# Three value blocks of one head group per layer, stored on forty partitions and loaded by eight five-row transfers

## The chip, the cores and the metric

The kernel runs on one core of one Trainium2 chip. The metric is the device time of one execution in microseconds, as the median of several runs; the kernel before takes 2583.27 us. A profile of one execution, with a record of every instruction and every DMA packet, is the source of all other numbers.

## What is computed

One decode step (one new token, batch of two) goes through two layers. Each layer is an attention block over a long key and value cache followed by a gated feed-forward block, and both layers use the same caches and weights:

```
x = x + attention(layernorm(x), k_cache, v_cache, wq, wo)   # 32 query heads, 8 key heads, 32768 keys, 128 wide, float32
x = x + ((relu(h @ W_gate) * (h @ W_up)) @ W_down), h = layernorm(x)
(both lines once more)

q = (h @ wq) as [2, 32 heads, 1, 128];  scores = q . k / sqrt(128);  p = softmax(scores);  o = p . v;  o @ wo
```

The caches are 2 x 8 x 32768 x 128 floats each, 268 MB for the keys and 268 MB for the values. They do not fit on the chip's on-core memory, so each layer reads all of them.

## The kernel before

**Tiling.** There are 16 head groups (8 key heads times 2 batch rows). A group's keys are two tiles of 128 partitions x 16384 floats (8 MB each), its values as well. Such a tile is four pages of 128 x 4096 floats (2 MB), and a page is eight blocks of 128 x 512 floats, so a group has 8 pages and 64 value blocks. Layer 0 takes the groups in order 0 to 15, layer 1 from 15 to 0.

**Loop.** In a layer, step i multiplies the queries with the keys of group i (`keys(i)`, matmuls at line 219 into `sc`), then the probabilities of group i-1 with its values (`values(i-1)`, line 263 into `acc`). The softmax of group i is split: `soft_max` (line 227) after the first value page, `soft_tail` (line 242: transposes the probabilities to `pT`, sums them) after the second key page of the next step. `head_out` and `project` add a group's output through `wo` to `op`. After group 15 come the feed-forward block (`wgu`, `wd`) and, in layer 0, the queries of layer 1 (`wq`).

**Memory and loads.** All loaded data and most scratch live in one tile, `arena`, 220 units of 1 KB per partition. `take` picks the free units that have been free longest, `done` gives units back. A load (line 73) is one DMA that SyncE (SP) issues in program order; each waits until the work that used its units has ended. Besides, a load waits for the eighth load before it: there are eight completion semaphores (DMAHW0 to DMAHW7 in the order of the program), used in turn, and one is used again only when its last transfer has landed on all sixteen DMA engines. A load of 8 MB is usually issued two or three tiles ahead of its use. A tile with 128 rows is spread evenly over the 16 DMA engines, eight rows each.

**Ends of the layers.** Layer 0 keeps the keys of its last group, and some pages of its values, for layer 1, which starts with the same group; the arena has then less room, and the values of its last two groups are loaded in pages of 2 MB (or 16 KB per row), not tiles of 8 MB. In layer 1 only the very last group's values are loaded in pages. `selq` is a small constant (128 rows of 128 bytes), loaded near the end of layer 0 by six transfers of 2, 3, 5, 6, 7 and 105 rows (lines 409 to 411).

Of the kernel before, what the change touches and what calls it, by code (L numbers as in the profile page):

```python
# [7 lines left out]
F32 = mybir.dt.float32  # L8
# [4 lines left out]
P = 128  # L13
D = 512
HKV, REP, DH, SK = 8, 4, 128, 32768
NB = 2
F = 1792
NG = HKV * NB
NT = 8
# [5 lines left out]
NLAYER = 2  # L25
# [12 lines left out]
KEPT_PART, KEPT_FROM = 3, 6  # L38
DOWN = (4, 4, 2, 2, 1, 1)

C_SAME, C_MEAN, C_SELH, C_PAIR, C_COL, C_SELQ, C_END = 0, 128, 256, 272, 304, 306, 338

SELQ_ROWS = (0, 2, 5, 10, 16, 23, 128)


@with_exitstack
def attention_reglu_decode(ctx: ExitStack, tc: tile.TileContext, x, k, v, wq, wo, wgu, wd, consts, out):
# [53 lines left out]

    xq = sb.tile([P, P], F32, name="x")
    nc.scalar.dma_start(xq, x)
    cst = sb.tile([P, C_SELQ], F32, name="cst")
    nc.scalar.dma_start(cst, consts[:, :C_SELQ])
    selq = sb.tile([P, C_END - C_SELQ], F32, name="selq")
    same = cst[:, C_SAME : C_SAME + P]
    selh = cst[:, C_SELH : C_SELH + 16]
    pair = cst[:, C_PAIR : C_PAIR + 32]
    mean_rows = cst[:, C_MEAN : C_MEAN + P]  # L110
    col = cst[:, C_COL : C_COL + NB]

    mean_cols = sb.tile([P, 1], F32, name="ones")
# [7 lines left out]
    acc = ps.tile([P, D], F32, name="acc")  # L121
# [86 lines left out]
        nc.vector.tensor_copy(qz[:, i % 2, 28 : 28 + REP], qT[:, REP * hk : REP * hk + REP, b])  # L208


    sc_of, pT_of, linv_of, red_of = {}, {}, {}, {}

    def k_tile(L, i, n, j, kt):
        if j == 0:
# [24 lines left out]
        nc.scalar.activation(p[0], sc_of[n].rearrange("p a b -> p (a b)"), AF.Exp, bias=nm[:, 0:1], scale=1.0, accum_out=rs)  # L239
        red_of[n] = (p, rs)  # L240

    def soft_tail(L, n):
        p, rs = red_of.pop(n)
        pT = take(2 * D)
        for B in range(2):
            nc.vector.transpose(pT[0][:, B * D : (B + 1) * D], p[0][:, B * D : (B + 1) * D])  # L246
        done(p)
        sm = small(f"sm{L}_{n}")
        nc.tensor.matmul(sm[:, 0:1], same, rs, start=True, stop=True)  # L249
        linv = one()  # L250
        nc.vector.reciprocal(linv, sm[:, 0:1])  # L251
        pT_of[n], linv_of[n] = pT, linv

# [93 lines left out]
    for L in range(NLAYER):  # L347
        last = L == NLAYER - 1
        seq = list(range(NG)) if L % 2 == 0 else list(range(NG - 1, -1, -1))

        def keys(i):
            n = seq[i]
            if i < NG - 1:
                place_queries(i + 1, seq[i + 1])
            if last and i == 0:
                loads = list(kept_k)
                kept_k.clear()
            else:
                loads = pages(k, n, not (last and i == 1))
            for j, t in enumerate(loads):  # L360
                k_tile(L, i, n, j, t[0])
                if not last and i == NG - 1:
                    kept_k.append(t)
                else:
                    done(t)
                if last and i == 0:
                    yield
                if j == 1 and i >= 1:
                    soft_tail(L, seq[i - 1])
                if j == 2 and i >= 2:  # L370
                    head_out(L, seq[i - 2])
                    if i % 2 == 1:
                        project(load(wo[seq[i - 2] // NB], True), i == 3, False)


        def values(i, soft):
            n = seq[i]
            whole = (j for j in ())
            if i == NG - 1:
                pieces = [(j, 0, 8, None) for j in range(NT - 1)]  # L380
                pieces += [(NT - 1, h, h + 2, None) for h in range(0, 8, 2)]
                if not last and KEPT_FROM < 8:
                    pieces[KEPT_PART : KEPT_PART + 1] = [(KEPT_PART, 0, KEPT_FROM, None), (KEPT_PART, KEPT_FROM, 8, None)]
            elif last and i == 0:
                pieces = kept_v[1:] + kept_v[:1]
                pieces += [(j, 0, 8 if j != KEPT_PART else KEPT_FROM, None) for j in range(NT) if j not in KEPT_PAGES]
                kept_v.clear()
            else:
                pieces = [(j, 0, 8, None) for j in range(NT)]
                whole = pages(v, n, last or i < NG - 2)  # L390
            for at, (j, lo, hi, t) in enumerate(pieces):
                t = t or next(whole, None) or load(v[n, j // HALF, :, j % HALF * PAGE + lo * D : j % HALF * PAGE + hi * D])
                v_tile(n, j, t[0], at == 0, j == NT - 1, range(lo, hi))
                if not last and i == NG - 1 and (j in KEPT_PAGES or j == KEPT_PART and lo):
                    kept_v.append((j, lo, hi, t))
                else:
                    done(t)
                if soft is not None and at == 0:
                    soft_max(L, soft)
            evacuate(L, n, i == NG - 1)  # L400

        first_keys = keys(0)
        queries(L, total, seq[0], first_keys if last else iter(()))
        list(first_keys)
        soft_max(L, seq[0])
        for i in range(1, NG):
            list(keys(i))
            values(i - 1, seq[i])
            if i == NG - 2 and not last:
                for lo, hi in zip(SELQ_ROWS, SELQ_ROWS[1:]):  # L410
                    nc.sync.dma_start(selq[lo:hi], consts[lo:hi, C_SELQ:])
        soft_tail(L, seq[NG - 1])
        head_out(L, seq[NG - 2])
        values(NG - 1, None)
# [48 lines left out]
```

## Time and profile before

| | us |
|---|---|
| median of three runs (2582.8 to 2583.68) | 2583.27 |
| the profiled execution | 2581.4 |
| its span, first to last instruction | 2579.5 |
| TensorE busy (matmul) | 1299.9 |
| VectorE busy | 143.5 |
| time of DMA packets on the main queue, as a share of 16 engines over the span | 99.5% |

The span is what the trace shows; the profiled execution has 1.9 us around it, and it is 1.9 us under the median. The profile's views used here are the page, the chain of work that ended last, tables of stretches (busy time, DMA share), the timeline, what SP's queue waited for, and DMA packets by queue in a stretch. The DMA share of a stretch is the mean busy share of the 16 DMA engines; packets are counted in the stretch in which they start, so a share can stand a little over 1.

### The profile page before, as it was taken

How to read it: one execution, taken by the hardware profiler on the slowest of the kernel's cores; microseconds unless marked ns; L12 is line 12 of the kernel's file. 1: busy time of each engine (PE TensorE's matmuls, PEld its weight loads, DVE VectorE, ACT ScalarE, POOL GpSimd, SP SyncE). 2: the span in 40 equal slices, each digit the busy share in tenths (PEclk: the TensorE clock that was granted, in tenths of full speed). 3: DMA queues.
4: the chain of work that ended last, by engine and by line, in shares of the span. 5: the costliest groups of instructions: out<-in, count | busy, mean ns of one | idle time of the engine just before them, and what ended most of it. 6: DMA issues, size and time to landing. Idle time of an engine off the chain costs nothing.

```text
span 2579.5 us, 20070 instructions
## 1 busy us (share of the span) xinstructions
PE 1299.9 (50%) x9544; PEld 343.3 (13%) x9544; DVE 143.5 (6%) x341; ACT 42.0 (2%) x69; POOL 3.0 (0%) x11
## 2 busy tenths in 40 slices
PE   2554554455445444545575554445445544554456
PEld 0111111111111111111111111111111101111111
DVE  0000000000000000000010000000000000000000
ACT  0000000000000000000000000000000000000000
POOL 0000000000000000000000000000000000000000
PEclk9777777777777777777878677777777776777778
DMA  9999999999999999999999999999999999999998
GB/s 425 428 434 434 432 429 435 431 435 431 428 438 434 425 437 434 430 431 427 407 409 436 432 433 431 433 435 427 434 436 428 432 436 430 432 432 432 435 424 371
DMA packets 30776, 1107.33 MB, mean 429 GB/s; under 512 B 3558, under 2 KB 3942, under 8 KB 7142
## 3 DMA queue, kind: packets, MB, share of 16 engines
q1 hardware_dynamic: 30406, 1105.82, 99.5%
q8 instruction: 75, 1.23, 0.2%
q10 hardware_dynamic: 288, 0.22, 0.0%
q14 instruction: 7, 0.06, 0.0%
HBM read 1105.96 MB, written 0.07 MB: 429 GB/s over the span
## 4 chain that ended last, share of the span: by engine, by line
DMA 67%; PE 23%; another core or an unknown queue 10%; issue 0%; DVE 0%; ACTq 0%; SPq 0%; DVEq 0%
DMA arena<-k 54%; PE sc L219 16%; DMA arena<-v 7%; PE acc L263 5%; DMA cst<-consts 2%; DMA arena<-wgu 1%; DMA arena<-wd 1%; PE po L287 1%; DMA arena<-wq 1%; PE op L169 1%; PE qp L189 1%; PE mp L233 0%; PE sm L249 0%; PE gu L306 0%
## 5 line engine op out<-in xcount | busy, mean ns | idle before, releaser
L263 PE MATMUL acc<-arena 128*16 128x512 f32 x4136 | 587.7, 720 | 606.4 <-DMA arena<-v 606.3
L219 PE MATMUL sc<-arena,qz 128*32 128x512 f32 x4096 | 590.2, 728 | 592.9 <-DMA arena<-k 592.9
L219 PEld LDWEIGHTS sc<-arena,qz 128*32 128x32 f32 x4096 | 144.0, 130 | 986.0 <-issue 668.4
L263 PEld LDWEIGHTS acc<-arena 128*16 128x16 f32 x4136 | 119.2, 109 | 1025.7 <-DMA arena<-v 513.5
L229 DVE TENSOR_REDUCE stat<-sc 128x1 f32<-128x1024 f32 x32 | 39.2, 1225 | 656.9 <-PE sc L219 656.9
L239 ACT ACTIVATE arena<-sc,stat 128x1024 f32<-128x1024 f32 x32 | 35.6, 1113 | 2374.0 <-DVE stat L236 2322.1
L281 DVE TENSOR_SCALAR arena<-acc,stat 128x512 f32<-128x512 f32 x30 | 22.5, 751 | 732.9 <-PE acc L263 732.9
L246 DVE STREAM_TRANSPOSE arena<-arena 128x512 f32<-128x512 f32 x64 | 41.5, 687 | 2.5 <-ACT arena L239 2.5
L287 PE MATMUL po<-cst,arena 128*128 128x4 f32 x256 | 33.9, 255 | 2.4 <-DVE arena L278 1.2
L287 PEld LDWEIGHTS po<-cst,arena 128*128 128x128 f32 x256 | 31.1, 191 | 27.0 <-issue 23.5
L251 DVE RECIPROCAL stat<-sm 128x1 f32<-128x1 f32 x32 | 5.3, 166 | 422.6 <-PE sm L249 422.6
L306 PE MATMUL gu<-arena 128*32 128x448 f32 x128 | 23.3, 840 | 10.7 <-DMA arena<-wgu 9.9
L236 DVE TENSOR_REDUCE stat<-mp 128x1 f32<-128x32 f32 x32 | 6.1, 192 | 358.0 <-PE mp L233 358.0
L189 PE MATMUL qp<-arena 128*32 128x512 f32 x128 | 20.1, 735 | 8.3 <-DMA arena<-wq 6.7
L142 PE MATMUL meana<-stat,cst 128*128 128x1 f32 x4 | 0.9, 304 | 43.4 <-DMA cst<-consts 42.9
L233 PEld LDWEIGHTS mp<-arena,cst 128*128 128x128 f32 x64 | 13.0, 253 | 52.1 <-issue 45.3
L169 PE MATMUL op<-arena,oT 128*2 128x128 f32 x512 | 17.7, 281 | 4.1 <-DVE oT L290 4.1
L233 PE MATMUL mp<-arena,cst 128*128 128x32 f32 x64 | 16.9, 352 | 3.2 <-DVE arena L232 3.2
L249 PEld LDWEIGHTS sm<-stat,cst 128*128 128x128 f32 x64 | 9.5, 188 | 27.6 <-issue 27.6
L169 PEld LDWEIGHTS op<-arena,oT 128*2 128x2 f32 x512 | 12.1, 86 | 6.0 <-DVE oT L290 5.5
L249 PE MATMUL sm<-stat,cst 128*128 128x1 f32 x64 | 12.2, 260 | 0.0
L290 DVE COPY oT<-po 128x4 f32<-128x4 f32 x32 | 5.2, 161 | 77.2 <-PE po L287 77.2
(51 smaller groups left out, 71.2 us busy)
## 6 DMA issues: line engine op xcount, KB each, us to landing
arena<-v SPq DMA_DIRECT2D x25, 2048.0 KB, 34.3
arena<-wo SPq DMA_DIRECT2D x16, 1024.0 KB, 50.5
arena<-k SPq DMA_DIRECT2D x8, 2048.0 KB, 14.2
arena<-wq SPq DMA_DIRECT2D x8, 1024.0 KB, 7.1
arena<-wgu SPq DMA_DIRECT2D x8, 896.0 KB, 8.5
arena<-wgu SPq DMA_DIRECT2D x4, 1792.0 KB, 21.0
arena<-v SPq DMA_DIRECT2D x9, 512.0 KB, 28.0
arena<-wd SPq DMA_DIRECT2D x4, 1024.0 KB, 7.8
```

The source lines that it names most:

```text
L169: nc.tensor.matmul(tot[32 * c : 32 * c + rows.shape[-1], :P], rows, w[:, c * P : (c + 1) * P], start=start, stop=stop)
L189: nc.tensor.matmul(qp[32 * c : 32 * c + 32, B, :], xT[:, kt, :], t[0][:, c * D : (c + 1) * D], start=kt == 0, stop=kt == KT - 1)
L219: nc.tensor.matmul(sc_of[n][32 * c : 32 * c + 32, B, :], qz[:, i % 2, 28 - 4 * j : 60 - 4 * j], kt[:, ch * D : (ch + 1) * D], start=j == 0 ...
L229: nc.vector.tensor_reduce(m1, sc_of[n], AX.XY, ALU.max)
L233: nc.tensor.matmul(mp[:, :32], same, mt[0], start=True, stop=True)
L239: nc.scalar.activation(p[0], sc_of[n].rearrange("p a b -> p (a b)"), AF.Exp, bias=nm[:, 0:1], scale=1.0, accum_out=rs)
L246: nc.vector.transpose(pT[0][:, B * D : (B + 1) * D], p[0][:, B * D : (B + 1) * D])
L249: nc.tensor.matmul(sm[:, 0:1], same, rs, start=True, stop=True)
L263: nc.tensor.matmul(acc[32 * c : 32 * c + 16, e * w : (e + 1) * w], pT[:, B, m, 16 * J : 16 * J + 16], vt[:, at * D + e * w : at * D + (e + ...
L281: nc.vector.tensor_scalar_mul(acs, acc, linv[:, 0:1])
L287: nc.tensor.matmul(po[:, :REP], acs[0][:, t * P : (t + 1) * P], selh[:, 4 * t : 4 * t + 4], start=t == 0, stop=t == 3)
L306: nc.tensor.matmul(gu[32 * j : 32 * j + 32, s, :FS], xT[:, kt, :], t[0][:, j * FS : (j + 1) * FS], start=kt == 0, stop=kt == KT - 1)
```

## The change

In each layer one group (the one at step 14 of 16, `i == NG - 2`) has three of its 64 value blocks taken out of the ordinary layout: blocks 4, 5 and 6 of page 3. Their 384 keys, padded to 400, are stored a second time in a new input, `side`, as 40 rows of 20,480 bytes: ten chunks of 40 keys. They stand on partitions 0 to 19 and 32 to 51 of the arena, and eight transfers of five rows (every fourth partition) load them, between the first and the second page of that group. Page 3 is then loaded in two parts, blocks 0 to 3 and block 7. The group's other pages are loaded one by one in both layers (in layer 1 they were two tiles of 8 MB).

The probabilities of these keys need another layout as well: `side_keys` makes it in `soft_tail` of that group with three transposes and one multiplication on VectorE and one memset on GpSimd, and `v_side` adds ten matmuls into `acc` after the first value page. `selq` becomes a part of `cst`, and its six transfers go.

```diff
-SELQ_ROWS = (0, 2, 5, 10, 16, 23, 128)
+SIDE_PAGE, SIDE_AT, SIDE = 3, 4, 3
+SIDE_ROWS, SIDE_CHUNKS = 20, 5
...
-    cst = sb.tile([P, C_SELQ], F32, name="cst")
-    nc.scalar.dma_start(cst, consts[:, :C_SELQ])
-    selq = sb.tile([P, C_END - C_SELQ], F32, name="selq")
+    cst = sb.tile([P, C_END], F32, name="cst")
+    nc.scalar.dma_start(cst, consts)
...
-    def soft_tail(L, n):
+    def soft_tail(L, n, aside=False):
...
+        if aside:
+            side_of[n] = side_keys(p[0])
...
+    def side_keys(p):
+        W = SIDE_CHUNKS * 32
+        t = take(2 * W)
...
+        nc.gpsimd.memset(t[0][64:, W:], 0.0)
+        nc.vector.transpose(chunks(t[0][:, :W]), windows(p))
+        for c in (0, 32):
+            nc.vector.transpose(chunks(t[0][c : c + 32, W:]), windows(p[64 + c : 96 + c]))
+        nc.vector.tensor_scalar_mul(t[0], t[0], side_rows[:, 0:1])
+        return t
+
+    def v_side(n, vt):
+        t = side_of.pop(n)
+        J = SIDE_PAGE // 4
+        for k in range(2 * SIDE_CHUNKS):
+            nc.tensor.matmul(
+                acc[32 * (k % 4) : 32 * (k % 4) + 16, :],
+                t[0][:, 32 * k + 16 * J : 32 * k + 16 * J + 16],
+                vt[:, k * D : (k + 1) * D],
+                start=False, stop=False,
+            )
+        done(t)
+
+    def load_side(n):
+        t = take(2 * SIDE_CHUNKS * D, False, False)
+        for c in (0, 32):
+            for r in range(4):
+                nc.sync.dma_start(t[0][c + r : c + SIDE_ROWS : 4], side[n, c // 32, r])
+        return t
...
+            elif i == NG - 2:
+                pieces = [(0, 0, 8, None)]
+                for j in range(1, NT):
+                    if j == SIDE_PAGE:
+                        pieces += [(j, 0, SIDE_AT, None), (j, SIDE_AT + SIDE, 8, None)]
+                    else:
+                        pieces.append((j, 0, 8, None))
...
+                if i == NG - 2 and at == 1:
+                    t_side = load_side(L)
+                    v_side(n, t_side[0])
+                    done(t_side)
...
-            if i == NG - 2 and not last:
-                for lo, hi in zip(SELQ_ROWS, SELQ_ROWS[1:]):
-                    nc.sync.dma_start(selq[lo:hi], consts[lo:hi, C_SELQ:])
```

SP's order near the end of layer 0, from the last whole tiles on, with the semaphores that each load waits for. Before:

```order
L73 DMA arena<-k 128x16384 [waits DMAHW1_49,PE_49]
L73 DMA arena<-wo 128x2048 [waits DMAHW2_49]
L73 DMA arena<-k 128x16384 [waits DMAHW3_49,PE_49]
L73 DMA arena<-v 128x4096 [waits DMAHW4_49,PE_49]
L73 DMA arena<-v 128x4096 [waits DMAHW5_49,PE_49]
L73 DMA arena<-v 128x4096 [waits DMAHW6_49,PE_49]
L73 DMA arena<-v 128x4096 [waits DMAHW7_49,PE_49]
```

And now:

```order
L75 DMA arena<-k 128x16384 [waits DMAHW3_49,DMAHW0_49,PE_49]
L75 DMA arena<-wo 128x2048
L75 DMA arena<-k 128x16384 [waits DMAHW1_49,PE_49]
L75 DMA arena<-v 128x4096 [waits DMAHW2_49,PE_49]
L296 DMA arena<-side 5x5120 [waits DVE_49,PE_49]
L296 DMA arena<-side 5x5120 x3
L296 DMA arena<-side 5x5120 [waits DMAHW3_49,DVE_49]
L296 DMA arena<-side 5x5120 [waits DMAHW4_49]
L296 DMA arena<-side 5x5120 [waits DMAHW5_49]
L296 DMA arena<-side 5x5120 [waits DMAHW6_49]
L75 DMA arena<-v 128x4096 [waits DMAHW7_49,PE_49]
L75 DMA arena<-v 128x4096 [waits DMAHW0_49,PE_49]
```

Eight more loads stand between the first page of values and the second. The fifth to the eighth wait in turn for the last `k`, `wo`, `k` and `v` loads above them (the semaphore of the eighth, DMAHW6, is that of the first page), and the second page waits for the first side transfer.

TensorE's order at the same place, from the second half of the last keys on. Before:

```order
L219 MATMUL sc_15_2440<-arena,qz 32x512 x40
L263 MATMUL acc<-arena 16x512 x8
L233 MATMUL mp_15_2544<-arena,cst 128x32
L263 MATMUL acc<-arena 16x512 x56
L249 MATMUL sm_15_2615<-stat,cst 128x1
```

And now:

```order
L222 MATMUL sc_15_2433<-arena,qz 32x512 x40
L308 MATMUL acc<-arena 16x512 x8
L236 MATMUL mp_15_2542<-arena,cst 128x32
L284 MATMUL acc<-arena 16x512 x10
L308 MATMUL acc<-arena 16x512 x20
L308 MATMUL acc<-arena 16x128 x4
L308 MATMUL acc<-arena 16x512 x32
L254 MATMUL sm_15_2632<-stat,cst 128x1
```

Ten matmuls on the side rows (line 284) follow the first page and the small `mp`; of page 3, four whole blocks and one block in four narrow parts are left. Layer 1 has the same sequence at its step 14.

## Rows read from the trace of the kernel before

**Rows 1.** The page: span, DMA queues (packets, MB, share of 16 engines), chain by engine.
```profile
span 2579.5 us, 20070 instructions
...
PE 1299.9 (50%) x9544; PEld 343.3 (13%) x9544; DVE 143.5 (6%) x341; ACT 42.0 (2%) x69; POOL 3.0 (0%) x11
...
q1 hardware_dynamic: 30406, 1105.82, 99.5%
q8 instruction: 75, 1.23, 0.2%
...
DMA 67%; PE 23%; another core or an unknown queue 10%; issue 0%; DVE 0%; ACTq 0%; SPq 0%; DVEq 0%
```

**Rows 2.** Table of stretches; the last three columns are PEclk, DMA share, GB/s.
```profile
100.00:1200.00 1100.00, 549.09 (x3976) 145.35 (x3976) 56.24 (x125) 16.86 (x28) 0.00 (x0) 0.74 1.00 433
1215.00:1260.00 45.00, 28.84 (x204) 6.45 (x196) 3.73 (x8) 1.21 (x2) 0.00 (x0) 0.85 1.01 427
1284.50:1289.50 5.00, 3.01 (x40) 0.88 (x32) 0.48 (x1) 0.39 (x1) 0.00 (x0) 1.00 0.52 213
2568.50:2573.00 4.50, 2.96 (x20) 0.51 (x16) 1.33 (x2) 0.00 (x0) 0.00 (x0) 0.70 0.52 215
```

**Rows 3.** Chain of work that ended last: end of layer 0, then end of the kernel.
```profile
1266.89 20.97 DMA arena<-v
1287.86 0.04 issue
...
2537.90 20.99 DMA arena<-wgu
2558.89 0.02 issue
2558.91 17.29 DMA arena<-wd
2576.20 0.04 issue
```

**Rows 4.** Packets starting in 1159.5 to 1161, 1161.3 to 1165.7 and 1165.5 to 1166.5 us.
```profile
DMA packets 113, 0.60 MB, mean 399 GB/s; under 512 B 104, under 2 KB 104, under 8 KB 104
...
DMA packets 24, 1.57 MB, mean 357 GB/s; under 512 B 0, under 2 KB 0, under 8 KB 0
...
DMA packets 87, 0.60 MB, mean 597 GB/s; under 512 B 78, under 2 KB 78, under 8 KB 78
```

**Rows 5.** Code loads: 0-1214.3, 1214.3-1290, 1310-2474.5, 2474.5-2577, last 1192.5-1194.5 us.
```profile
q8 instruction: 33, 0.54, 0.2%
...
q8 instruction: 3, 0.05, 0.3%
...
q8 instruction: 34, 0.56, 0.2%
...
q8 instruction: 4, 0.07, 0.3%
...
q8 instruction: 1, 0.02, 3.4%
```

**Rows 6.** Timeline of TensorE, value pages of layer 0 (start, us, engine, line, work).
```profile
1228.95 2.84 PE L263 MATMUL acc<-arena 128*16 128x512 f32 x16 [2.99 <-DMA arena<-v]
1233.84 3.26 PE L263 MATMUL acc<-arena 128*16 128x512 f32 x16 [2.05 <-DMA arena<-v]
```

**Rows 7.** What SP's queue waited for between 1190 and 1222 us.
```profile
SPq L73 <- DMA arena<-v: 18.3, 1, 18.3
```

**Rows 8.** Timeline, SP's issues: before that wait, after it, and the six selq.
```profile
1195.61 0.33 SPq L73 DMA_DIRECT2D arena<-v  x1
...
1219.87 0.33 SPq L73 DMA_DIRECT2D arena<-v  x1
...
1120.25 7.97 SPq L411 DMA_DIRECT2D selq<-consts  x6
```

**Rows 9.** Page, DMA issues: the store at the end, us from issue to landing.
```profile
out<-x SPq DMA_DIRECT2D x1, 64.0 KB, 1.5
```

**Rows 10.** Table of stretches, as in Rows 2, where the selq rows were moved.
```profile
1155.00:1160.00 5.00, 1.76 (x20) 0.23 (x8) 0.00 (x0) 0.00 (x0) 0.00 (x0) 1.00 0.98 411
1160.00:1166.00 6.00, 0.00 (x0) 0.00 (x0) 0.00 (x0) 0.00 (x0) 0.00 (x0) 0.63 0.99 427
```

More of the change, by code (lines that the diff above doesn't have):

```diff
@@ L39, with attention_reglu_decode @@
 DOWN = (4, 4, 2, 2, 1, 1)
-C_SAME, C_MEAN, C_SELH, C_PAIR, C_COL, C_SELQ, C_END = 0, 128, 256, 272, 304, 306, 338
-SELQ_ROWS = (0, 2, 5, 10, 16, 23, 128)
+SIDE_PAGE, SIDE_AT, SIDE = 3, 4, 3
+SIDE_ROWS, SIDE_CHUNKS = 20, 5
+C_SAME, C_MEAN, C_SELH, C_PAIR, C_COL, C_SELQ, C_SIDE, C_END = 0, 128, 256, 272, 304, 306, 338, 339
 @with_exitstack
-def attention_reglu_decode(ctx: ExitStack, tc: tile.TileContext, x, k, v, wq, wo, wgu, wd, consts, out):
+def attention_reglu_decode(ctx: ExitStack, tc: tile.TileContext, x, k, v, side, wq, wo, wgu, wd, consts, out):
     nc = tc.nc
@@ L109, in attention_reglu_decode @@
     pair = cst[:, C_PAIR : C_PAIR + 32]
+    selq = cst[:, C_SELQ : C_SELQ + 32]
     mean_rows = cst[:, C_MEAN : C_MEAN + P]
+    side_rows = cst[:, C_SIDE : C_SIDE + 1]
     col = cst[:, C_COL : C_COL + NB]
@@ L208, in place_queries @@
         nc.vector.tensor_copy(qz[:, i % 2, 28 : 28 + REP], qT[:, REP * hk : REP * hk + REP, b])
-    sc_of, pT_of, linv_of, red_of = {}, {}, {}, {}
+    sc_of, pT_of, side_of, linv_of, red_of = {}, {}, {}, {}, {}
     def k_tile(L, i, n, j, kt):
@@ L252, in soft_tail, with windows, chunks @@
         pT_of[n], linv_of[n] = pT, linv
+    def side_keys(p):
+        W = SIDE_CHUNKS * 32
+        t = take(2 * W)
+        at = SIDE_PAGE // 2 % 2 * D + (SIDE_PAGE % 2 * 8 + SIDE_AT) * 32
+        def windows(rows):
+            return bass.AP(rows.tensor, rows.offset + at, [rows.ap[0], [SIDE_ROWS, SIDE_CHUNKS], [1, 32]])
+        def chunks(rows):
+            return rows.rearrange("p (k r) -> p k r", r=32)
+        nc.gpsimd.memset(t[0][64:, W:], 0.0)
[21 more added lines that the diff above has]
+        return t
     def v_tile(n, j, vt, first, last, blocks):
@@ L368, in keys @@
                 if j == 1 and i >= 1:
-                    soft_tail(L, seq[i - 1])
+                    soft_tail(L, seq[i - 1], i == NG - 1)
                 if j == 2 and i >= 2:
@@ L387, in values @@
                 kept_v.clear()
+            elif i == NG - 2:
[5 more added lines that the diff above has]
+                        pieces.append((j, 0, 8, None))
             else:
                 pieces = [(j, 0, 8, None) for j in range(NT)]
-                whole = pages(v, n, last or i < NG - 2)
+                whole = pages(v, n, True)
             for at, (j, lo, hi, t) in enumerate(pieces):
+                if i == NG - 2 and at == 1:
+                    t_side = load_side(L)
+                    v_side(n, t_side[0])
+                    done(t_side)
                 t = t or next(whole, None) or load(v[n, j // HALF, :, j % HALF * PAGE + lo * D : j % HALF * PAGE + hi * D])
@@ L434 @@
     cst[:, C_PAIR : C_PAIR + 32] = np.equal.outer(rows // 4, np.arange(32))
+    cst[:, C_SIDE] = (rows < 64) & (rows % 32 < SIDE_ROWS)
     cst[:, C_COL : C_COL + NB] = np.equal.outer(rows % 32, np.arange(NB))
@@ L442, in by_block, with side_blocks @@
         return con(w.reshape(4, KT, 32, -1).transpose(1, 0, 2, 3)).reshape(KT, P, -1)
+    def side_blocks(vc):
+        sets = []
+        J, B, m = SIDE_PAGE // 4, SIDE_PAGE // 2 % 2, SIDE_PAGE % 2 * 8 + SIDE_AT
+        for L in range(NLAYER):
+            n = NG - 2 if L % 2 == 0 else 1
+            keys = vc[n % NB, n // NB].reshape(2, 4, 2, 4, 512, DH)[J, :, B, :, 32 * m : 32 * (m + SIDE)]
+            rowsets = np.zeros((4, 4, SIDE_CHUNKS * SIDE_ROWS, DH), np.float32)
+            rowsets[:, :, : 32 * SIDE] = keys.transpose(1, 0, 2, 3)
+            t = rowsets.reshape(2, 2, 4, SIDE_CHUNKS, SIDE_ROWS // 4, 4, DH)
+            sets.append(t.transpose(1, 5, 4, 0, 3, 2, 6).reshape(2, 4, SIDE_ROWS // 4, -1))
+        return con(np.stack(sets))
     wq = con(a["A_wq"].reshape(D, 2, HKV * REP // 2, 4, 32).transpose(0, 1, 3, 2, 4)).reshape(D, -1)
@@ L448 @@
         "v": con(a["A_v_cache"].reshape(NB, HKV, 2, 4, 2, 4, 16, 32, DH).transpose(1, 0, 2, 5, 7, 4, 6, 3, 8)).reshape(NG, 2, P, SK // 2),
+        "side": side_blocks(a["A_v_cache"]),
         "wq": con(by_block(wq).reshape(KT, P, 2, -1).transpose(1, 2, 0, 3)).reshape(P, -1),
```

## The prediction

> **What bounds the kernel now.** I read the page first. The DMA packets of the main queue fill 99.5% of the sixteen engines' time, TensorE is busy for half of it, and the chain that ended last is DMA for two thirds [rows 1]. So the time is bytes over engines, plus the moments in which an engine that matters has nothing queued.
>
> The table of stretches then shows where those moments are. In the middle of a layer the share is 1.00. At the end of layer 0 it falls to 0.52 for 5 us, and at the end of the kernel to 0.52 again [rows 2]: half of the engines are done and the other half works on. The chain passes through just these last loads [rows 3]: what sets the time is the slower half. The packet counts show the split before the end as well. Small packets (the selq rows with their completions, and the completions of the tile ahead of them) are served in two clumps, 104 by 1161 us and 78 from 1165.5 us on, with none between [rows 4]. Eight engines lead the other eight by some 5 us.
>
> The lead has a visible source. All loads are spread evenly, but 75 code loads of 16 KB [rows 1] are not: if all fall on eight engines, 33 of them by 1214 us [rows 5] make four each and one fifth. One takes 3.4% of sixteen engines over 2 us, or 1.09 us, by itself [rows 5]; a lead of 5 us over four gives 1.25 us with what it does to the packet beside it. I take 1.3 us. That they alternate over just the eight late engines is inferred, since no view names an engine.
>
> **The change part by part.**
>
> *Bytes off the slow half.* Pages land 4.89 us apart [rows 6]. Three blocks are 3/8 of a page: every engine loses 1.84 us per layer. The side rows (8 rows of 20,480 bytes on each of five engines, 163,840 bytes against a page's 131,072) take 6.11 us there. If the five are among the eight ahead, this eats into their lead of 5 us, so the slow half is 1.84 us faster per layer and nobody is later than it. That alone is -3.7 us.
>
> *The wait that comes in.* There are eight completion semaphores. The eighth side transfer reuses that of the first value page, so SP can issue it only when this page has landed on all sixteen engines; the second page stands behind it. SP now waits there for this very page, too, from 1195.9 to 1214.2 us [rows 7, 8], but with four further pages already queued. In the changed kernel nothing else is queued for the eleven engines without side rows. So the slowest engine, which lands the page last, runs dry as well. It stands idle for: the end of its last packet to the semaphore, SP's wake (0.02 to 0.04 us, as the issue pieces of [rows 3]), one issue ahead (0.33 us [rows 8], some 0.38 with the gap), and the second page's issue to its first bytes. The first and the last of these together are the latency of a transfer: the small store takes 1.5 us from issue to landing [rows 9], of which 64 KB at full rate are 0.15. So 0.03 + 0.38 + 1.35 = 1.8 us per layer. Ends: 1.4 if the issue ahead costs nothing, 2.2 if a load from HBM starts later than a store. I take 1.8, since both parts have a row. The 1.84 us saved are spent here.
>
> *The new levelling.* Behind this wait all engines start the second page nearly together. Before, the engine with five code loads was the last, and the three code loads that follow in the layer [rows 5] fell on engines with four, which only drew level with it. Now the page's landing carries the fifth code load to all, and one of the three comes on top: +1.3 us. In layer 1 it is the same: 34 code loads before its side rows (four each, two with five), then four, the last of them too late to matter [rows 5]. Ends: 0 (the late code loads hit engines that have slack) and 1.4. I take 1.3 per layer, as the code loads are paced by TensorE's program, which the change hardly moves ahead of these points.
>
> *Pages for tiles in layer 1.* 433 GB/s with 64 KB rows against 427 with 16 KB rows [rows 2] are 0.5 us for 16.8 MB; the 4.89 us per page, eight times against 38.7 us, give 0.4 us. I take 0.4 (ends 0 and 0.5).
>
> *What is hidden.* The loads behind the wait need room: the fifth page waits for TensorE to end with the first. That took until 1219.87, 5.6 us after landing [rows 7, 8], and the ten side matmuls add two to three us (sixteen records of the same kind take 2.84 to 3.26 us [rows 6]). Until then the second and third pages and the rest of the fourth, 2.6 pages or 12.8 us, are in flight, so nothing runs dry twice. SP issues the first seven side transfers while the last keys and the first page are still moving; on the five engines they are 7/8 of 6.11 = 5.3 us, about the lead. TensorE gains ten matmuls, VectorE three narrow transposes and a multiplication per layer, against idle halves [rows 1]; if that cover were gone, it would be a few us. Removing the six selq transfers frees about 0.1 us.
>
> *Small transfers.* The six selq transfers, 0.2 to 13 KB each, left the DMA share at 0.98 and 0.99 where their rows were moved [rows 10]: queued small transfers cost no time between them. The Trainium skill (DMA: Bandwidth & Descriptors, "Rules for kernel authors") advises the opposite of this change: full 128-partition transfers of a MiB or more, and merging small ones; and its "Anatomy of one DMA" gives about 2.0 us fixed per transfer on another issuing path. Paid eight times in a row, that estimate would be 16 us per layer on the five engines; by the row it is none, and I go by the row.
>
> *Sum.* Layer 0: -1.84 + 1.8 + 1.3 = +1.3 us. Layer 1: the same + 0.4 = +1.7 us. Together +2.9 (1.26 + 1.66): the profiled execution of 2581.4 us would be 2584.3, and the median 2583.27, which is 1.9 us over it, becomes **2586.2 us**, +0.11%. With all ends against each other: 2 x (-1.84 + 1.4) = -0.9 to 2 x (-1.84 + 2.2 + 1.4) + 0.5 = +4.0, so 2582.4 to 2587.3. This kernel's measurement can tell 0.2%, 5.2 us, from no change; the forecast is "within 0.2%".
>
> **The rivals.**
>
> *The idle time is hidden* (the change does what its bytes say). If the slowest engine still had work when the first page landed, or the page landed on all at nearly one time, the slow half would keep its 1.84 us per layer: 2583.3 - 3.7 = 2579.6 us, -0.14%, still within 0.2%. For it speaks the size of the side rows, which match the lead. Against it: the order shows no load for eleven engines between the first and the second page.
>
> *One of the five engines is not ahead* (slower). Then it is the last at the first page, has 6.1 us of side rows behind it, and starts the second page that much later: -1.84 + 6.11 = +4.3 us per layer without any idle time, +5.6 with the levelling, so 2591.9 to 2594.5 us, +0.33 to +0.43%. It decides as soon as one of the five lags by more than some 2 us. The counts bear on it: the 104 early packets are eight tile completions, eight packets for each of a leading engines with rows of the last selq transfer, and two for each single row of the first five that was early, 8 + 8a + 2s. With a = 7, s is 20 of 23, so only three single rows were late. The five lowest shares hold 20 of these rows, the sixth and seventh three: that is the case in which all five lead. With a = 8, s is 16, and one or two of them lag. The first fits exactly.
>
> *Side transfers pay singly*. With 1.35 us of latency each, eight take 8 x (0.76 + 1.35) = 16.9 us on the five engines, some 8 us per layer more than the lead and the idle time cover: about 2600 us. [Rows 10] speak against it.
>
> **How the numbers follow.** Forecast (idle time paid, levelling in part or whole, within 0.2%): 0.75. Hidden: 0.10. One engine not ahead: 0.06. Paid singly: 0.03. The forecast's mechanism over its upper end (a longer restart, a second dry moment), past 5.2 us: 0.04. A gain over 5.2 us has no source, as the bytes give 3.7 at most: 0.02 for what I don't see. That makes faster 0.02, same 0.85, slower 0.13. The range goes from 2579.6, the hidden case, to 2588.6, over the forecast's upper end by a quarter of a layer's wait; it leaves out the slower rivals and half of the hidden case.
>
> **What would show it.** In the changed profile: SP's queue has a wait for `v` ahead of the eighth side transfer, and the DMA share falls for about two us right behind the landing of the first page, in both layers, to 5/16 or less; the gap at the end of layer 0 (0.52 over 5 us) is gone or much shorter; the last page of a layer lands about as late as before or one to two us later. If the dip is missing, the first rival holds. If five engines lag at the end (share near 0.3 for several us), the second does. The forecast is wrong if the median is under 2579 or over 2589 us.

## The result, and the profile after

The changed kernel takes 2588.84 us (median of 14 runs, 2586.62 to 2590.59) against 2583.27 us for the kernel before (14 runs, 2580.95 to 2585.21): ratio 1.0023, 95% interval 1.0016 to 1.0030, or +5.6 us. The prediction was 2586.2 us, +2.9, with a range to 2588.6. The sign is right, the forecast size is half of what came. The median lies 0.24 us over the range, and just under the 2589 us that the prediction named as its sign of being wrong.

The page of the changed kernel, the lines that answer to [rows 1]:

```profile
span 2587.7 us, 20209 instructions
...
PE 1316.8 (51%) x9584; PEld 347.5 (13%) x9584; DVE 146.0 (6%) x349; ACT 42.1 (2%) x69; POOL 3.4 (0%) x13
...
q1 hardware_dynamic: 31552, 1105.87, 99.3%
q8 instruction: 75, 1.23, 0.2%
...
DMA 64%; PE 24%; another core or an unknown queue 10%; issue 0%; DVE 0%; SPq 0%; ACTq 0%; DVEq 0%
```

Almost the same bytes move (1105.87 against 1105.82 MB), the code loads are still 75, and TensorE is still half idle. The main queue's share falls from 99.5 to 99.3%: the engines stand idle more. Where they do is in the table of stretches (as in [rows 2]: the stretch and its length in us, busy us of the engines from TensorE to GpSimd with the number of instructions, then PEclk, DMA share, GB/s); first the kernel before, then the changed one:

```profile
1211.50:1215.50 4.00, 4.00 (x36) 1.04 (x32) 0.00 (x0) 0.00 (x0) 0.00 (x0) 0.85 1.01 430
2476.50:2480.50 4.00, 3.25 (x32) 0.72 (x24) 0.67 (x1) 0.00 (x0) 0.00 (x0) 1.00 0.98 426
```

```profile
1211.50:1215.50 4.00, 4.00 (x28) 1.03 (x24) 0.00 (x0) 0.00 (x0) 0.00 (x0) 0.61 0.08 31
1284.50:1289.50 5.00, 4.13 (x32) 1.25 (x36) 0.00 (x0) 0.00 (x0) 0.00 (x0) 0.68 1.04 418
2476.50:2480.50 4.00, 4.00 (x36) 1.04 (x32) 0.00 (x0) 0.00 (x0) 0.00 (x0) 0.86 0.09 39
```

For 4 us in each layer the DMA share is 0.08 and 0.09, where it was 1.01 and 0.98. And the gap at the end of layer 0 (0.52 over 5 us in [rows 2]) is gone: 1.04. Both were in the prediction's list of what would show it; the dip is deeper and twice as long as forecast ("for about two us", "to 5/16 or less"). A part of its length is that the other engines wait for the last one: by the DMA packets from 1211.5 us on, three of 16 KB start one after the other 0.6 us apart, at 1211.7, 1212.3 and 1212.9 us, which reads as one engine still at work on the first page. What SP's queue waited for between 1190 and 1222 us (us in total, times, longest us), then its issues around 1214 us (the timeline), both of the changed kernel:

```profile
SPq L296 <- DMA arena<-k: 20.0, 1, 20.0
SPq L296 <- DMA arena<-v: 4.2, 1, 4.2
```

```profile
1178.16 36.51 SPq L296 DMA_DIRECT2D arena<-side  x8
1214.78 2.60 SPq L75 DMA_DIRECT2D arena<-v  x4
```

Line 296 is the side transfer. The fifth waited for a key page before this stretch; the seventh waits 20.0 us for a key page, the eighth a further 4.2 us for the first value page, and the second value page is issued behind it, at 1214.78 us. Where the kernel before waited [rows 7], four pages were queued behind the page that it waited for; here nothing is.

How much of it reaches the end of the layer is read at two places. In the kernel before TensorE started on the fifth value page at 1233.84 us [rows 6], and the last piece of layer 0 landed at 1287.86 us [rows 3]. In the changed kernel's timeline of TensorE, and in its chain of work that ended last:

```profile
1235.83 3.23 PE L308 MATMUL acc<-arena 128*16 128x512 f32 x16 [3.36 <-DMA arena<-v]
```

```profile
1269.84 20.61 DMA arena<-v
1290.45 0.04 issue
```

The fifth page comes 1.99 us later, although 1.84 us of bytes were taken out ahead of it: the dry moment with what belongs to it costs 3.83 us. From there to the last piece it is 54.62 us, where it was 54.02: 0.60 us more. Layer 0 ends 2.59 us later; the prediction had 1.26.

This is one execution, and its parts are not all fixed. In the run with the side blocks in layer 0 alone (below), whose layer 0 is the same, the fifth page comes 1.27 us later than in [rows 6], and the last piece lands at 1290.19 us, 2.33 later than in [rows 3]; its timeline of TensorE and its chain:

```profile
1235.11 3.62 PE L308 MATMUL acc<-arena 128*16 128x512 f32 x16 [4.26 <-DMA arena<-v]
```

```profile
1269.14 21.05 DMA arena<-v
```

So the dry moment is 3.83 us in one execution and 3.11 in the other, and what follows up to the last piece 0.60 and 1.06: the two together, 4.43 and 4.17 us, are firmer than the split. The span of the profiled execution is 8.2 us longer (2587.7 against 2579.5), more than the 5.6 of the medians. By the chains, 2.59 us of it are there at the last piece of layer 0, 5.06 when the value load of layer 1 that comes next on the chain has landed (1401.41 against 1396.35 us), and the last 3.1 come in the rest of layer 1. The 2.5 us in between, at the border of the layers, are 0.6 in the run with layer 0 alone and 1.5 in a run in which layer 0 is unchanged (the pages alone, below), so the change is not shown to be their cause.

### The profile page after: what moved, and what is told of

It reads as the page before. It is cut to its first block, busy times and chain, and to the rows that moved or that the text cites. A ratio compares the mean times of both kernels' runs of the same rounds, so it can differ in the third digit from the quotient of the medians.

```text
span 2587.7 us, 20209 instructions
## 1 busy us (share of the span) xinstructions
PE 1316.8 (51%) x9584; PEld 347.5 (13%) x9584; DVE 146.0 (6%) x349; ACT 42.1 (2%) x69; POOL 3.4 (0%) x13
## 3 DMA queue, kind: packets, MB, share of 16 engines
q1 hardware_dynamic: 31552, 1105.87, 99.3%
## 4 chain that ended last, share of the span: by engine, by line
DMA 64%; PE 24%; another core or an unknown queue 10%; issue 0%; DVE 0%; SPq 0%; ACTq 0%; DVEq 0%
DMA arena<-k 53%; PE sc L222 16%; DMA arena<-v 8%; PE acc L308 5%; DMA cst<-consts 2%; DMA arena<-wgu 1%; PE po L332 1%; PE op L172 1%; PE qp L192 1%; DMA arena<-wq 1%; PE gu L351 0%; PE dn L373 0%; PE mp L236 0%; PE sm L254 0%
## 5 line engine op out<-in xcount | busy, mean ns | idle before, releaser
L351 PE MATMUL gu<-arena 128*32 128x448 f32 x128 | 21.4, 782 | 13.2 <-DMA arena<-wgu 12.4
```

What stands on the lines that cost most here:

```text
L351: nc.tensor.matmul(gu[32 * j : 32 * j + 32, s, :FS], xT[:, kt, :], t[0][:, j * FS : (j + 1) * FS], start=kt == 0, stop=kt == KT - 1)
```

## The experiments

The theory is that the loss is the dry moment behind the first value page. The rivals were the side rows themselves on five engines, the edits beside them (pages for tiles, the selq rows), and a loss at the border of the layers. The kernel before ran beside each of them: at 2581.98 us beside the two halves, the wait alone, the pages and layer 1 alone; at 2582.36 beside six, seven, sixteen and the first run of one ahead of each load; at 2582.29 beside layer 0 alone, the second of these runs and the selq rows. Differences are of these medians, or, where it says "by the ratio", the ratio times 2582 us; the two can differ by some tenths of a us. Intervals are 95%.

**The side transfers in two halves.** Four ahead of the second page, four behind it (`load_side` takes the half to load).

```diff
...
                 if i == NG - 2 and at == 1:
-                    t_side = load_side(L)
+                    t_side = load_side(L, 0)
+                if i == NG - 2 and at == 2:
+                    load_side(L, 32, t_side)
                     v_side(n, t_side[0])
```

> The changed kernel with its eight side transfers split: four (partitions 0-19) ahead of the second value page as before, four (32-51) and the ten matmuls behind the second page. SP then never waits for the page that it queued last: when it waits for the first page, the second is queued on all sixteen engines. Same bytes, same rows, same matmuls. Theory (the loss is the dry moment behind the first page, and what it does to the queues behind it): the idle time and the levelling are gone, the 1.84 us of bytes per layer stay, pages for tiles in layer 1 cost 0.4: 2583.3 - 3.7 + 0.4 = 2580.0 us, between 2579 and 2581.5, ratio to before 0.9983 to 0.9993. Rival (the loss is in the side rows themselves: 6.1 us on five engines, more issues, more matmuls): the time stays near the changed kernel's, 2587 to 2590 us.

Measured: 2582.14 us (2578.46 to 2585.08), ratio 0.9997 (0.9988 to 1.0006). The loss of the changed kernel is gone, so the rival falls; but the gain that the theory gave is missing in the median. The executions spread over 6.6 us: four of eleven are at 2580.1 us or less, where the theory had 2580.0. In its profile TensorE reaches the fifth page of layer 0 at 1231.96 us, 1.88 us ahead of [rows 6], just the 1.84 of bytes; the last piece lands at 1286.61 us, 1.25 ahead. The dip is not gone but shallow: over the same 4 us the DMA share is 0.78 in layer 0 and 0.84 in layer 1, and the slower engines lose nothing by it up to the fifth page. What is lost later is taken up again under "What stays open".

**The wait alone.** The kernel before with eight tiny transfers (five rows of 32 bytes, read by nobody) between the first and second page, and pages for tiles in layer 1.

```diff
...
+    tiny = sb.tile([P, 8], F32, name="tiny")
...
-                whole = pages(v, n, last or i < NG - 2)
+                whole = pages(v, n, i < NG - 2)
...
+                if i == NG - 2 and at == 1:
+                    for r in range(0, 40, 5):
+                        nc.sync.dma_start(tiny[r : r + 5], consts[r : r + 5, C_SELQ : C_SELQ + 8])
```

> The kernel before with pages for tiles in the last group step but one of layer 1, and with eight tiny transfers of five rows (32 bytes each, of the constants, read by nobody) between the first and the second value page of that group step in both layers: the wait alone, without side rows, without bytes saved, without added matmuls. Theory (the wait costs the time): per layer an idle time of about 2.4 us on the engine that is last, as the trace of the changed kernel shows, and 1.3 us of levelling, and 0.4 for the pages: 2583.3 + 7.8 = 2591 us, ratio 1.0025 to 1.0037. If the changed kernel's +5.6 is taken and the bytes (3.7) are given back, the same kind of number follows: +9.3, 2592.6 us. Rival (the cost is in the side rows): nothing but eight issues, 2583.5 to 2585 us.

Measured: 2590.53 us (five runs, 2589.96 to 2592.6), ratio 1.0032 (1.0019 to 1.0045), +8.5 us. Without one side row or one block saved, the wait costs 4.1 us per layer (with 0.3 us taken off for the pages, below); by the interval, between 2.3 and 5.7. Its table of stretches has the same dip, and no gap at the end of layer 0 (1.01): the wait levels the two halves without any side rows. Its timeline has the fifth page 3.73 us later than [rows 6], and its chain shows what is on the path behind the wake of SP at 1214.06 us:

```profile
1211.50:1215.50 4.00, 4.00 (x28) 0.96 (x24) 0.00 (x0) 0.00 (x0) 0.00 (x0) 0.63 0.25 74
1284.50:1289.50 5.00, 3.49 (x39) 0.73 (x32) 0.00 (x0) 0.00 (x0) 0.00 (x0) 0.84 1.01 404
```

```profile
1237.57 2.94 PE L264 MATMUL acc<-arena 128*16 128x512 f32 x16 [2.98 <-DMA arena<-v]
```

```profile
1170.38 43.68 DMA arena<-v
1214.06 0.02 issue
1214.08 0.26 SPq L395
1214.34 0.05 issue
1214.39 0.02 SPq L73
1214.41 0.03 issue
1214.44 8.40 DMA arena<-v
```

The first page lands; 0.02 us later SP issues the eighth tiny transfer, in 0.26 us; then the second page, which lands 8.40 us after its issue. Queued behind another, a page lands 4.89 us after the one ahead [rows 6].

**Pages for tiles alone.** The second of the three edits above, without the first and the last.

> The kernel before with one edit: the values of the last group step but one of layer 1 come as eight pages and not as two tiles of four pages, as in the changed kernel. Theory: +0.4 us (0 to 0.5), 2583.7 us, ratio 1.0000 to 1.0003. Rival (this edit, which the sum priced lowest, carries the loss of layer 1): +2 to +4 us, 2585 to 2587 us, ratio 1.0008 to 1.0015.

Measured: 2582.25 us (2581.04 to 2585.0), ratio 1.0000 (0.9991 to 1.0009), +0.3 us. The rival's +2 us lies at the edge of the interval (-2.3 to +2.3); this edit carries no part of the loss that can be told.

**Layer 1 alone, layer 0 alone.** The changed kernel with the side blocks in one layer (both runs without the six selq transfers); for layer 1:

```diff
...
-            elif i == NG - 2:
+            elif last and i == NG - 2:
...
-                whole = pages(v, n, True)
+                whole = pages(v, n, last or i < NG - 2)
...
-                if i == NG - 2 and at == 1:
+                if last and i == NG - 2 and at == 1:
```

and for layer 0 `not last` in the same places, with the line on `whole` as in the changed kernel.

> The changed kernel with the side blocks in layer 1 alone; layer 0's values are loaded whole as before (the six selq transfers stay out). Theory (each layer pays its own wait, and layer 0's wait also sets what happens at the border of the layers): layer 1 alone costs -1.84 + 2.4 + 1.3 + 0.4 = +2.3 us, 2585.5 us, ratio 1.0006 to 1.0011. Rival (the border of the layers costs its 2.7 us because the ends of layer 0 are levelled in any case, or by the missing selq transfers): +5, 2588 us, ratio 1.0018 or more. Second rival (the layers are not independent, layer 1 makes back its part when layer 0 is undisturbed): 2582 to 2583.5 us.

Measured for layer 1: 2585.16 us (2583.28 to 2588.14), ratio 1.0013 (1.0004 to 1.0021), +3.2 us.

> The changed kernel with the side blocks in layer 0 alone; layer 1 as before, its values in tiles of four pages. Theory (each layer pays for its own wait: 3.0 us of idle time and 1.5 us of code loads on top, less 1.84 us of bytes, as the landings of the changed kernel show): +2.6 us against the kernel before, +2 to +3.5; with the run of layer 1 alone (ratio 1.0013, +3.3 us) the two add up to the changed kernel's +5.6 to 6. Rival (the layers are not independent, or the border of the layers carries a loss of its own that belongs to layer 0): +4.5 us or more; or 0, if layer 1 makes it up.

Measured for layer 0: 2585.11 us (2582.87 to 2586.77), ratio 1.0010 (1.0002 to 1.0019), +2.8 us. Together +6.0, the changed kernel's +5.6 within what these runs can tell. Each layer pays for itself. The intervals, +1.0 to +5.4 us and +0.5 to +4.9, are too wide to rule out a border loss of a us or two, and the first rival of the run with layer 1 alone (+5 us) is inside its interval; against it stands the profile, in which the end of layer 0 is as before (gap share 0.57, the last piece 0.24 us ahead of [rows 3]). In the chain of the run with layer 1 alone the eighth side transfer stands on the path:

```profile
2433.35 42.33 DMA arena<-v
2475.68 0.02 issue
2475.70 0.66 SPq L296
2476.36 0.06 issue
2476.41 0.02 SPq L75
2476.43 0.03 issue
2476.46 0.38 SPq L75
```

From the first page's landing at 2475.68 to the second page's issue at 2476.46 are 0.78 us, of which the issue of the side transfer takes 0.66.

**Six before, two behind.** The split is moved to the point at which SP, ahead of the second page, no longer waits for the first.

```diff
...
                 if i == NG - 2 and at == 1:
-                    t_side = load_side(L)
+                    t_side = load_side(L, range(6))
+                if i == NG - 2 and at == 2:
+                    load_side(L, range(6, 8), t_side)
```

> The changed kernel with the order six side transfers, second value page, two side transfers, ten matmuls, third page. SP then waits ahead of the second page only for the last key page, which lands 4.9 us before the first value page. Theory (the dry moment is the price): no idle time on the last engine; the bytes give -1.84 us per layer and the code loads behind it take 0 to 1.4 back: -3.3 to 0 us against the kernel before. The split four and four came out at 0. Rival (lost lead, side rows): as the changed kernel, +5 to +6 us.

Measured: 2582.72 us (2580.83 to 2587.13), ratio 1.0004 (0.9995 to 1.0013). The dip is gone in both layers (DMA share 0.99 and 1.02), and with it most of the loss; the gain is missing here too.

**Seven before, one behind.** As above with 7 in place of 6. The second page itself now waits for the first.

> The changed kernel with seven side transfers ahead of the second value page and the eighth behind it: now the second page itself waits for the first page's completion, and nothing is issued between. Theory (idle time = SP's wake, the issue of the eighth side transfer of 0.76 us, and 2.2 us from the second page's issue to the first of its bytes): only the 0.76 us per layer go, +4.1 us against the kernel before where the changed kernel has +5.6. Rival (the eighth transfer's own latency is part of the wait): the time falls by 2 us or more per layer, to +1.5 or less.

Measured: 2587.73 us (2586.23 to 2589.49), ratio 1.0019 (1.0010 to 1.0028), +4.9 us by the ratio. One transfer more ahead of the second page than in the kernel just above costs 4 us by the ratios (5.0 by the medians), and the rival (+1.5 or less) falls. Its chain has the wait without an issue between:

```profile
1213.66 0.02 issue
1213.67 0.02 SPq L75
1213.69 0.03 issue
1213.72 7.73 DMA arena<-v
```

7.73 us from issue to landing, 2.84 more than between two queued pages: this restart is the larger part of the price, and the eighth issue the smaller. Its 0.76 us per layer can't be told in the time (1.0 us less than the changed kernel by the ratios, 0.2 by the medians, where 1.5 were expected).

**Sixteen transfers.** Each side transfer in two by columns.

```diff
             for r in range(4):
-                nc.sync.dma_start(t[0][c + r : c + SIDE_ROWS : 4], side[n, c // 32, r])
+                for lo, hi in ((0, D), (D, 2 * SIDE_CHUNKS * D)):
+                    nc.sync.dma_start(t[0][c + r : c + SIDE_ROWS : 4, lo:hi], side[n, c // 32, r][:, lo:hi])
```

> The changed kernel with each side transfer cut in two by columns (2,048 and 18,432 bytes a row): the same rows and bytes in sixteen transfers. The eighth again waits for the first value page, and eight more issues stand between it and the second page. Theory (idle time counts the issues between the wake and the second page): 8 x 0.7 = 5.6 us per layer on top, 11 us on top of the changed kernel, +15 to +18 us against the kernel before. Rival (the cost goes with the bytes of the side rows and the five engines): as the changed kernel, +5 to +7 us.

Measured: 2599.95 us (five runs, 2598.73 to 2604.22), ratio 1.0071 (1.0057 to 1.0084), +18.3 us by the ratio (+17.6 by the medians). The same bytes to the same rows, and by the ratios 12.4 us more than the changed kernel: 6.2 us per layer for eight more issues. SP's timeline, the chain and TensorE's timeline show where:

```profile
1209.42 11.21 SPq L297 DMA_DIRECT2D arena<-side  x10
1220.73 1.32 SPq L75 DMA_DIRECT2D arena<-v  x3
```

```profile
1220.73 8.03 DMA arena<-v
```

```profile
1242.10 3.61 PE L309 MATMUL acc<-arena 128*16 128x512 f32 x16 [4.63 <-DMA arena<-v]
```

The second page is issued at 1220.73 us, 5.95 later than in the changed kernel, and the fifth page comes 6.27 us later. The rival falls: what counts is how late the second page is issued, not the bytes of the rows.

**One side transfer ahead of each of eight loads.** SP never waits for the last page that it queued. The expectation says that four pages stand ahead in the queue; by SP's timeline it is less: when the first page lands, the second, the third and the first part of the fourth are queued behind it, two and a half pages.

```diff
...
-                if i == NG - 2 and at == 1:
-                    t_side = load_side(L)
-                    v_side(n, t_side[0])
-                    done(t_side)
+                if i == NG - 2 and 1 <= at <= 8:
+                    t_side = load_side(L, at - 1, t_side if at > 1 else None)
+                    if at == 8:
+                        v_side(n, t_side[0])
+                        done(t_side)
```

> The changed kernel with one side transfer ahead of each of the next eight loads, and the ten matmuls ahead of the last page's: four pages stand ahead in the queue as in the kernel before. Theory (the dry moment is the price): no dip behind the first page, no levelling of the two groups of engines; -3.3 us against the kernel before, -0.5 at worst. Rival (side rows on five engines cost by themselves): +2 us or more.

Measured: 2579.63 us (2577.73 to 2581.07), ratio 0.9987 (0.9978 to 0.9996). Once more:

> The kernel with one side transfer ahead of each of the next eight loads once more, in other executions, since its gain of 0.13% is near what can be told from nothing. Theory: the bytes alone, 2 x -1.84 + 0.3 = -3.4 us, ratio 0.9980 to 0.9993. Rival (the first result was a draw of fast executions): ratio 0.9995 to 1.0005.

Measured: 2579.42 us (2577.93 to 2582.27), ratio 0.9988 (0.9979 to 0.9996). Both the changed kernel and the kernel before are beaten: by the ratios -3.4 and -3.1 us against the kernel before (-2.7 and -2.9 by the medians; intervals -5.7 to -1.0 and -5.4 to -1.0), which is what the bytes alone give. In the first run's profile its table of stretches, TensorE's timeline, and its chain at the end of layer 0:

```profile
1211.50:1215.50 4.00, 4.00 (x28) 0.93 (x24) 0.00 (x0) 0.00 (x0) 0.00 (x0) 0.57 1.01 428
2476.50:2480.50 4.00, 4.00 (x40) 1.10 (x32) 1.47 (x2) 0.00 (x0) 0.00 (x0) 1.00 0.97 392
```

```profile
1231.94 2.76 PE L307 MATMUL acc<-arena 128*16 128x512 f32 x12 [4.30 <-DMA arena<-v]
```

```profile
1267.19 19.10 DMA arena<-v
1286.30 0.04 issue
```

No dip in either layer; the fifth page comes 1.90 us ahead of [rows 6], the last piece 1.56 us ahead of [rows 3] (2.02 and 1.83 in the second run's profile). The gap at the end of layer 0 is closed here too (1284.5 to 1289.5 us: 1.02), without a wait: the side rows close it as well, so in the changed kernel the closed gap is no sign of the wait.

**The selq rows alone.** The kernel before with the 32 columns loaded with the other constants.

```diff
-    cst = sb.tile([P, C_SELQ], F32, name="cst")
-    nc.scalar.dma_start(cst, consts[:, :C_SELQ])
-    selq = sb.tile([P, C_END - C_SELQ], F32, name="selq")
+    cst = sb.tile([P, C_END], F32, name="cst")
+    nc.scalar.dma_start(cst, consts)
...
-            if i == NG - 2 and not last:
-                for lo, hi in zip(SELQ_ROWS, SELQ_ROWS[1:]):
-                    nc.sync.dma_start(selq[lo:hi], consts[lo:hi, C_SELQ:])
```

> The kernel before with one edit of the change: the 32 selq columns come with the other constants in one load at the start, and the six selq transfers in layer 0 are gone. Theory: their rows cost nothing to speak of, -0.1 us (-0.5 to +0.5). Rival (taking them out frees SP and the queue earlier, and this has hidden a part of the loss in the changed kernel): -2 us or less.

Measured: 2582.76 us (2580.77 to 2584.84), ratio 1.0003 (0.9994 to 1.0012): no difference that can be told, and the rival (-2 us or less) falls.

## Why the prediction was half right

**The bound and the bytes: right.** The -1.84 us per layer is borne out. The kernel with spread side transfers gains 3.4 and 3.1 us by the ratios, and the fifth page comes 1.90 and 2.02 us earlier in its two profiles, 1.88 with four and four; in profiles with an unchanged layer 0 it comes between 0.29 us earlier and 0.37 later. The first rival's -3.7 us (-0.14%) is, within the interval, what a kernel without the wait gives: -3.4 and -3.1.

**The wait: the right mechanism, the wrong size.** This is the step that failed. The sum had 1.8 us for it (0.03 for the wake, 0.38 for the issue ahead, 1.35 for the second page's start), with an upper end of 2.2. The runs show some 3.2 without a code load in it (0.03, 0.76 and 2.4):

- The issue ahead: 0.76 us with its gap, not 0.38. The 0.33 us came from a load of 128 rows [rows 8]. A side transfer of five rows takes twice that, as the view of its sixteen records in the changed kernel says (minimum, median, maximum in ns):

```profile
L296 SPq DMA_DIRECT2D arena<-side x16: 657/659/838, 1178.2 to 2479.2; - x16
```

- The restart: 1.35 was taken from the 64 KB store [rows 9]. With seven before, in layer 1, SP issues the second page at 2478.56 us and TensorE starts on it at 2485.86; no code load falls in between. That is 7.3 us, 2.4 more than the 4.89 between two queued pages. Its timeline, and the busy share of the DMA engines in forty slices of 0.19 us from 2478.5 us on (in tenths):

```profile
2478.56 0.35 SPq L75 DMA_DIRECT2D arena<-v  x1
```

```profile
2485.86 1.91 PE L308 MATMUL acc<-arena 128*16 128x512 f32 x16 [0.76 <-DMA arena<-v]
```

```profile
DMA  0000099300099829849988992984988899699298
```

Nothing moves for 0.9 us; then come 262 KB, which is sixteen packets of 16 KB; then nothing for some 0.6 us; only 2.0 us after the issue do the engines run at full rate. The wait alone has the same pattern: 0.9 us in layer 1, then 262 KB, and 7.3 us in all. In layer 0 the restart takes 7.73 (seven before) and 8.40 us (the wait alone), 2.8 and 3.5 over 4.89, each with one code load in it. In the run of sixteen no code load starts there, yet it takes 8.03; there side rows still move beside the page. What one code load adds is thus not separated, and how much of the restart each of the sixteen engines loses, no view shows.

The dry moment as a whole came to 3.83 and 3.11 us in layer 0 (from the fifth page, two profiles), and to 3.73 in the kernel with the wait alone.

**The levelling: its size holds roughly, its place can't be separated.** The sum had 1.3 us of code loads on top. Behind the fifth page 0.60 and 1.06 us are lost in layer 0; a code load that falls into the restart is inside the dry moment. Wait and levelling together are 4.43 and 4.17 us, where the prediction had 3.1. Of the 1.1 to 1.3 us that are missing, 0.4 is the issue; the restart without a code load has 1.0 more than the 1.35. As an estimate, the prediction's sum with 0.76 and 2.4 in place of 0.38 and 1.35 gives 4.5 us. Layer 1, measured alone, is +3.2 us against +1.66 in the sum; the same two terms, and the interval of that run (+1.0 to +5.4 us) allows no finer reading. That eight of the engines lead because the code loads fall on the other eight stays inferred: no run tries it.

**Pages for tiles, and the six selq transfers:** priced at +0.4 and -0.1, measured +0.3 and +0.5, each with an interval of about 2.3 us to both sides: no term of any weight, as the sum had it.

**The rivals.** *Hidden* falls with the dips. *One of five engines not ahead* falls, since with spread transfers the same rows go to the same partitions and nothing is lost to them. *Side transfers pay singly* falls in its form (2.1 us each, some 8 us per layer), but not wholly: behind the wake SP's issues are paid one by one, 6.2 us for eight more by the times, 0.78 us each. The Trainium skill (DMA: Bandwidth & Descriptors, "Anatomy of one DMA") gives about 2.0 us fixed per transfer on another issuing path. The prediction's estimate from that figure was 16 us for eight; by the run of sixteen the price is that of the issue alone, and only where nothing else is queued. The prediction's row for it [rows 10] was one of queued transfers, and stood for them rightly.

**The range** ended at 2588.6, 1.3 us over the forecast's upper end; the prediction calls this a quarter of a layer's wait, but a quarter of 1.8 us is 0.45. The upper end of 2.2 us for the wait was built from a store's latency plus a reserve, though a page of 2 MB and a store of 64 KB are far apart. A nearer row was there: the first load of the kernel before, the 8 MB of `wq`, is issued at 0.74 us onto idle engines. It lands 22.1 us later, where four pages of 2 MB in a full queue take 19.6, so this start cost some 2.5 us more:

```profile
arena<-wq SPq DMA_DIRECT2D x1, 22.1
```

**What stays open.** The two kernels with the second page ahead of the last side transfers (four and four, six and two) have a shallow dip and none, yet reach 2582.1 and 2582.7 us instead of some 2579.5, with a wide spread. Their profiles are of executions well over these medians, 2584.8 us (the second longest of eleven) and 2587.13 (the longest), so they show what is lost there and not in the median. Two things are seen in them; neither was tried by itself.

With six and two the fifth page of layer 0 comes at 1234.25 us, 0.41 later than in [rows 6] in spite of the bytes saved. When the last two side transfers are issued only one page is queued; a possible reading, not shown, is that the lead of the eight engines is then used up and side rows meet engines without slack, as in the second rival.

In both, more is lost at the border of the layers, where TensorE is on the path. From the landing of the last piece of layer 0 to that of the next value load on the chain in layer 1 the kernel before takes 108.5 us, the two runs with spread transfers 108.8 and 108.7, the pages alone 110.0, but four and four 112.9 and six and two 112.1. The table of stretches with four and four, and then that of the kernel before:

```profile
1280.00:1286.00 6.00, 3.61 (x40) 0.76 (x40) 0.00 (x0) 0.00 (x0) 0.00 (x0) 1.00 1.02 410
1286.50:1291.50 5.00, 3.98 (x40) 2.66 (x44) 0.64 (x2) 0.48 (x1) 0.00 (x0) 0.50 1.00 391
```

```profile
1280.00:1286.00 6.00, 4.27 (x40) 0.73 (x32) 0.00 (x0) 0.00 (x0) 0.00 (x0) 0.92 0.88 360
1286.50:1291.50 5.00, 3.36 (x56) 2.02 (x56) 0.65 (x2) 0.47 (x1) 0.00 (x0) 0.97 0.71 254
```

Where TensorE multiplies the last value piece and projects it (1286.5 to 1291.5 us), its granted clock is 0.50, the lower level of 1.2 GHz, after six us at 1.00 in which it was busy for 3.61; in the kernel before it is 0.97 there, after 0.92 with 4.27 us busy. From 1291.5 to 1300 us the granted clock is 0.50 with four and four and with six and two, and between 0.58 and 1.00 in the other eleven profiles. There is one profile of each of these two kernels, so whether this differs from execution to execution, and makes the wide spread, is not shown.

## What to carry to other kernels

Count what is queued behind the transfer that the issuing engine waits for, not only the bytes: with eight completions in use, eight small transfers in a row used up the whole queue, and the engines ran dry although in one run they carried 160 bytes each. With one small transfer between two large ones they cost nothing here that the runs could tell. And price a restart from a row of a large load on idle engines (the first load of a kernel is one), or leave its upper end open when there is none.

## What the runs showed of the hardware that was not expected

The time of a transfer's issue on SP does not follow its number of rows: five rows of 20,480 bytes take 0.66 us, 128 rows of 16,384 bytes 0.33 us [rows 8], five rows of 32 bytes 0.27 us (the median of sixteen in the run with the wait alone). Nor does it follow their bytes: in the run of sixteen, five rows of 2,048 bytes take 0.66 us as well (the least of its 32 records is 0.657). The side rows go to every fourth partition and the others to neighbouring ones; whether that is the reason was not tried. A page of 2 MB that starts on idle engines lands 7.3 to 8.4 us after its issue, 2.4 to 3.5 us more than one that is queued; in the profiles above sixteen packets come first, then a pause. And sixteen transfers that are too small to fill the engines cost their issue time one after the other: in the kernel with sixteen, the DMA share stays at 0.26 for 5.5 us behind the dip:

```profile
1211.50:1215.50 4.00, 4.00 (x24) 0.91 (x20) 0.00 (x0) 0.00 (x0) 0.00 (x0) 0.57 0.05 20
1215.50:1221.00 5.50, 5.50 (x54) 1.42 (x46) 1.47 (x2) 0.00 (x0) 0.00 (x0) 1.00 0.26 76
```
